# Putting VectorE and ScalarE into program order from item 3 on, with one piece of side work behind each part of the first product

## The chip, the cores and the metric

The kernel runs on one core of a Trainium2 chip. The core has a matrix engine (TensorE, PE in the profile; its weight loads are listed as PEld), three engines for elementwise work (VectorE or DVE, ScalarE or ACT, GpSimd or POOL) and SyncE (SP), which issues most of the transfers. All engines run at the same time, each through its own list of instructions in order, and wait for each other by semaphores. The metric is the time of one execution on the device in microseconds (us), as the median of several runs.

## The reference

A channel attention over four batches gives a matrix of 14592 rows of 256, and a mixture of 16 experts is applied to it: each row goes to one expert, picked by two softmaxes.

```python
B, N, C = (4, 3648, 256)
qn = q / (np.linalg.norm(q, axis=1, keepdims=True) + 1e-06)
kn = k / (np.linalg.norm(k, axis=1, keepdims=True) + 1e-06)
s = kn.transpose(0, 2, 1) @ qn / tau
a = softmax(s); x = (v @ a).reshape(B * S, D)
...
for g in range(G):            # 4 groups
    for e in range(Eg):       # 4 experts in each
        h = np.maximum(xg[mask_e] @ w1[g, e], 0.0)     # 256 -> 1024
        ye = h @ w2[g, e]                              # 1024 -> 256
        out[tok_idx] = combined[:, None] * ye
```

Everything is fp32, and the output is one row of 256 for each of the 14592 tokens.

## The kernel before

The first quarter of the time computes the attention and the routing, and scatters each row of x with its weight and token number into a table in HBM that is sorted by expert. This stage is not touched by the change.

The rest is the experts. The rows of an expert are cut into *items* of 512 rows; there are 28 (`NBIG`), numbered i = 0 to 27. An item loads its expert's w1 and w2 (1 MB each, tiles `wraw`) and its rows (`xg`). For the accuracy of fp32 each operand is split into a rounded high part and the rest (`wh`, `wl`, `xth`, `xtl`, `hh`, `hl`), and each product is made of three matmuls: high by high, high by low, low by high. Splitting a weight takes a ScalarE copy (`wh`, line 637) and a VectorE subtraction (`wl`, line 638) for each half of 128x1024.

An item has eight *parts* f = 0 to 7 of 128 hidden channels. For each part `ffn1` (line 772) multiplies the rows by a part of w1 with six matmuls of 512 columns into `hmm`; ScalarE makes `hh` from it (line 776) and VectorE `hl` (line 777). `ffn2` (line 788) multiplies that part by w2 with twelve matmuls of 256 columns into two accumulators `yacc`. It runs two parts behind (`lag`): after the first product of part f comes the second product of part f - 2. So two parts into the next item an item is finished: ScalarE and VectorE evacuate an accumulator each (`ys`, lines 795 and 797) and GpSimd scatters the rows to `out` (line 798).

Beside the parts of item i the kernel prepares item i + 1: its w1 and w2 are split (`split_w`), its rows are turned (`turn_x`, line 659, a VectorE transposition from tile `xq` to `xT`) and split (`split_x`, lines 667 and 668). Item i + 2's rows are fetched by an indirect gather on GpSimd and brought into blocks by 16 small transfers on SyncE (`quads_of`, line 615, tile `xq`). Items below 4 (`KPRE`) turn their rows with TensorE instead.

Items 4 to 27 each also *host* a stage of a small product for rows left over after the items (`q_...`): four experts' rows of 32 at a time, in a cycle of four items, so that j % 4 = 0 and 1 are the first product's two stages (`qmm`, line 875) and 2 and 3 the second's (`qacc`, line 892). The stage runs in part 2. Its weights are 1 MB more for each item, in two tiles of four loads (lines 856 and 859). All weights go through one ring of three staging tiles `wraw`, in the order w2, two tiles for the small product, w1 of the item after: each load waits until the tile three before it has been used.

The order of instructions on an engine comes from a list scheduler, which goes by the order of the program, by priorities and by its own estimate of times. `tc.manual_schedule` takes engines out of that: they run in program order. Before the change SyncE, GpSimd and TensorE are so ordered from item 3 on (lines 1002 to 1004: n counts parts, UN0 is 4), while VectorE and ScalarE are ordered by the scheduler.

Of the kernel before, what the change touches and what calls it, by code (L numbers as in the profile page):

```python
# [18 lines left out]
B, NT, C = 4, 3648, 256  # L19
# [18 lines left out]
KPRE = 4  # L38
NBIG = N // BIG
# [18 lines left out]
def attention_moe(ctx: ExitStack, tc, q, k, v, tau, w_group, w_expert, w1, w2, out):  # L58
# [19 lines left out]
    def ring(*shape, name):  # L78
        return rp.tile([P, *shape], F32, tag="ring", name=name, bufs=RING)
# [36 lines left out]
    slot4 = cp.tile([P, 4], F32, name="slot4")  # L116
# [14 lines left out]
    part = cp.tile([P, 1], F32, name="part")  # L131
# [344 lines left out]
    def tokens(ids, row, slot, nv, behind=None):  # L476

        keep = hp.tile(list(slot.shape), I32, tag=f"keep{slot.shape[1]}", name="keep", bufs=2)
        DVE.tensor_scalar(keep, slot, nv, -1.0, ALU.is_lt, ALU.mult)
        ins = DVE.tensor_tensor(ids, row.bitcast(I32), keep, ALU.bitwise_and)  # L480
        if behind is not None:
            tc.add_manual_dep(ins.ins, behind.ins.name,
                              mybir.DependencyInfo(mybir.DependencyClass.NoSync, mybir.DependencyReason.DATA),
                              reason="the rows are there by then")
        DVE.tensor_scalar(ids, ids, -1.0, float(NOID), ALU.mult, ALU.add)
# [124 lines left out]
    def quads_of(d):  # L610

        d["xq"] = ring(16, C // 4, name="xq")
        for q in range(4):
            for s in range(4):
                SP.dma_start(d["xq"][q * 32:(q + 1) * 32, s::4, :],  # L615
                             d["xg"][s * 32:(s + 1) * 32, :, q * 64:(q + 1) * 64])

    ET = mybir.EngineType
# [18 lines left out]
        ACT.activation(whs[n][:, s], raw[:, s], AF.Copy)  # L637
        DVE.tensor_tensor(wls[n][:, s], raw[:, s], whs[n][:, s], ALU.subtract)  # L638

    def split_w(i, which):  # L640

        if not whs:
            for n in range(4):
                for l, nm in ((whs, "wh"), (wls, "wl")):
                    l.append(wp.tile([P, 2048], F32R, name=f"{nm}{n}", bufs=1) if n < 3 else None)
        if i == 1 and which == "w2":
            wq = ctx.enter_context(tc.tile_pool(name="wq", bufs=1, side="right"))
            whs[3], wls[3] = [wq.tile([P, 2048], F32R, name=nm, bufs=1) for nm in ("wh3", "wl3")]
        d = items[i]
        raw = d.pop(which + "r")  # L650
        n = 2 * (i % 2) + (which == "w2")
        for c in range(2):
            split_half(raw.rearrange("p c f -> p (c f)"), n, c)
        for k, t in (("h", whs[n]), ("l", wls[n])):
            d[which + k] = t.rearrange("p (c f) -> p c f", c=raw.shape[1])

    def turn_x(d):
        d["xT"] = ring(2, BIG, name="xT")
        DVE.transpose(d["xT"].rearrange("p c (t b) -> p t c b", b=32),
                      d["xq"].rearrange("p t (a c) -> p t c a", c=2))  # L660

    def split_x(d):
        w = BIG
        xh = tp.tile([P, 2, w], F32R, tag="th", name="xth")
        xl = tp.tile([P, 2, w], F32R, tag="tl", name="xtl")
        if "xT" in d:
            ACT.activation(xh, d["xT"], AF.Copy)
            ins = DVE.tensor_tensor(xl, d["xT"], xh, ALU.subtract)
        for c in range(2) if "xT" not in d else ():
            tr = ps.tile([P, 512], F32, tag="tr", name="xtr")  # L670
            for t in range(4):
                PE.transpose(tr[:, t * P:(t + 1) * P], half(d["xg"][:, t, 0:C], c), ident)
            ACT.activation(xh[:, c, :], tr[:, :w], AF.Copy)
            ins = DVE.tensor_tensor(xl[:, c, :], tr[:, :w], xh[:, c, :], ALU.subtract)  # L674
        d["xh"], d["xl"] = xh, xl
        d["ids"] = hp.tile([P, 4], I32, tag="ids", name="ids", bufs=4)
        tokens(d["ids"], d["xg"][:, :, C], slot4, d["nv"], None if d is items[0] else ins)

    items = [dict() for _ in range(NBIG)]

# [19 lines left out]
    for t in range(len(xs_at)):  # L700
# [38 lines left out]
        if x == UX - 2:  # L739
            split_w(0, "w1")  # L740
# [25 lines left out]
    def ffn1(d, f):  # L766
        mm = ps.tile([P, 512], F32, tag="mm", name="hmm", bufs=3)
        fs = slice(f * P, (f + 1) * P)
        n = 0
        for c in range(2):  # L770
            for wt, xt in ((d["w1h"], d["xh"]), (d["w1h"], d["xl"]), (d["w1l"], d["xh"])):
                PE.matmul(mm, wt[:, c, fs], xt[:, c, :], start=(n == 0), stop=(n == 5))  # L772
                n += 1
        hh = hp.tile([P, 512], F32R, tag="hh", name="hh")
        hl = hp.tile([P, 512], F32R, tag="hl", name="hl")
        ACT.activation(hh, mm, AF.Relu)  # L776
        d["hl"] = DVE.scalar_tensor_tensor(hl, mm, 0.0, hh, ALU.max, ALU.subtract)  # L777
        d["h", f] = hh, hl
# [34 lines left out]
    def fetch_big(i, which):  # L813
        d, tb, k = where(i)
        fetch_w(d, tb, k, which)
# [47 lines left out]
    def q_xT(q, behind):  # L863
        pxt = ps.tile([P, 512], F32, tag="tr", name="qxt")
        for c in range(2):
            PE.transpose(pxt[:, c * P:(c + 1) * P], half(qs["xg"][q % 2][:, 0:C], c), ident)
        ACT.activation(qs["xT"][q % 2].rearrange("p c n -> p (c n)"), pxt[:, 0:2 * P], AF.Copy)
        tokens(qs["ids"][q % 2], qs["xg"][q % 2][:, C:C + 1], slotq, tb_pc[1][:, q:q + 1], behind)
# [126 lines left out]
    for n in range(len(seq) + lag):  # L995
        if n == 1:
            fetch_w(items[1], tb_pre, 1, "w1")
            fetch_w(items[1], tb_pre, 1, "w2")
        if n == 2:
            ms.close()  # L1000
            ms.enter_context(tc.manual_schedule(engines={ET.SP, ET.Pool}))
        if n == 8 * (UN0 - 1):
            ms.close()
            ctx.enter_context(tc.manual_schedule(engines={ET.SP, ET.Pool, ET.PE}))
        if n < len(seq):
            i, f = seq[n]
            j, jn = host(i), host(i + 1)
            if f == 3:
                if i + 2 == KPRE:
                    advance(1000)  # L1010
                    scatter(NJ)
                    tb_big, tb_pc, tb_sub, nsub = tables_rest()
                get(i + 2, weights=jn is None)
                if jn is not None:
                    if jn == 0:
                        q_tiles()
                    if jn % 4 == 0:
                        q_rows(jn // 4)
                    q_weights(jn // 4, jn % 4, 0)
            if jn is not None and f == 5:  # L1020
                q_weights(jn // 4, jn % 4, 1)
            if f == 5 and KPRE <= i + 2 < NBIG:
                quads_of(items[i + 2])
            if jn is not None and f == 7 and i + 2 < NBIG:
                fetch_big(i + 2, "w1")
            if j is not None and f == 1 and i + 1 < NBIG:
                fetch_big(i + 1, "w2")
            if j is not None and j % 4 == 0 and f == 1:
                q_xT(j // 4, items[i]["hl"])
            if i + 1 < NBIG:  # L1030
                if f == 2 and i + 1 >= KPRE:
                    turn_x(items[i + 1])
                if f == 3:
                    split_x(items[i + 1])
                if f == (4 if j is None else 5):
                    split_w(i + 1, "w1")
                if f == (6 if j is None else 7):
                    split_w(i + 1, "w2")
            if i == NBIG - 1 and f == 4:
                ns = nc.values_load(nsub[0:1, 0:1], min_val=0, max_val=NSUB)  # L1040
            ffn1(items[i], f)
            if j is not None:
                q, k = j // 4, j % 4
                if f == 2:
                    (q_ffn1 if k < 2 else q_ffn2)(q, k % 2)
                if f == 4 and k < 2:
                    q_hT(q, k)
                if f == 3 and k == 3:
                    q_put(q)
        if lag <= n < len(seq):  # L1050
            i, f = seq[n - lag]
            ffn2(items[i], f)
            if f == 7:
                finish(items[i])
        if n == len(seq) + lag - 1:

            d = items[NBIG - 1]
            d["ys"] = ring(4, C, name="ys")
            for t in (0, 2, 1, 3):
                for f in range(8 - lag, 8):  # L1060
                    ffn2(d, f, [t])
                put(d, t, d["acc"][t // 2][:, t % 2, :], t // 2)
        if n >= 1:
            advance(20 if n >= 3 else 1)
            scatter(8)
# [86 lines left out]
```

## Time and profile before

| | us |
|---|---|
| median of 3 runs | 1013.89 |
| lowest and highest | 1009.99, 1016.67 |
| the profiled execution | 1012.64 |
| its span, first to last instruction | 1010.6 |
| start of items 0, 3, 4, 8, 27 (first matmul) in the span | 257.8, 332.1, 358.4, 458.1, 968.7 |

A profile row of a group or a time line gives the engine, the line of the kernel, the operation, what it writes and reads (out<-in) and its shape; in a time line the start and duration stand ahead, and in brackets the idle time of the engine before it with what ended that wait. A row of windows gives the length of a stretch and for each engine its busy time with the number of instructions in it, then the granted clock of TensorE, the share of time in which the 16 DMA engines were busy, and GB/s. Start to start, a matmul of 512 columns takes 0.23 us there and one of 256 columns 0.12 us, though each is listed as longer: they overlap.

### The profile page before, as it was taken

What the parts mean: (1) busy time and instruction counts of PE and PEld (TensorE: products, weight loads), DVE (VectorE), ACT (ScalarE), POOL (GpSimd) and SP (SyncE); (2) the same over time, 40 slices, a digit from 0 to 9 for tenths busy, and PEclk for the clock granted to TensorE, in tenths of its full rate; (3) what the DMA queues carried; (4) which work ended last, traced back from release to release, by engine and by line L of the source; (5) the groups of instructions that cost most, each with busy time, mean ns of one, the idle gap of its engine ahead of it and who ended that gap; (6) DMA issues with size and microseconds to landing.
All of it is one profiled execution on the core that took longest, in us unless ns stands there. A gap on an engine that the chain in (4) does not pass through costs nothing.

```text
span 1010.6 us, 17899 instructions
## 1 busy us (share of the span) xinstructions
PE 952.6 (94%) x6238; PEld 819.8 (81%) x6238; DVE 612.9 (61%) x1159; ACT 472.3 (47%) x740; POOL 329.4 (33%) x425
## 2 busy tenths in 40 slices
PE   7999999988899999999999999999999999999994
PEld 6888988978788888888778777788778887777884
DVE  6989978786899555444445555554545444555551
ACT  6777677454544344334433444444443333344431
POOL 0005868886785222121112211121112111211111
PEclk9999999988999999999999999999999999999998
DMA  8857777366663466676566666676667766666650
GB/s 297 328 201 247 263 258 263 118 207 244 206 232 124 154 209 211 227 234 195 184 204 204 226 219 215 224 236 224 209 212 236 230 222 201 206 202 213 198 184 25
DMA packets 160884, 214.53 MB, mean 212 GB/s; under 512 B 65331, under 2 KB 119355, under 8 KB 160784
## 3 DMA queue, kind: packets, MB, share of 16 engines
q1 hardware_dynamic: 144352, 168.73, 51.5%
q0 software_dynamic: 14944, 44.54, 12.2%
q8 instruction: 51, 0.84, 0.3%
q14 instruction: 49, 0.40, 0.1%
q10 hardware_dynamic: 1488, 0.02, 0.1%
HBM read 170.33 MB, written 31.39 MB: 200 GB/s over the span
## 4 chain that ended last, share of the span: by engine, by line
PE 59%; DVE 9%; ACT 3%; issue 3%; DMA 2%; SPq 1%; POOL 1%; POOLq 0%; DVEq 0%; ACTq 0%
PE hmm L772 26%; PE yacc L788 25%; DVE wl L638 5%; PE qmm L875 2%; PE qacc L892 2%; PE xmm L307 2%; ACT wh L637 2%; ACT hh L776 1%; SPq L615 1%; DMA wraw<-in_moe_w 1%; DVE hl L777 1%; DMA x_sorted<-xs,si 1%; PE qtr L882 1%; DMA xg<-x_sorted,ix_big 0%; POOL out L798 0%
## 5 line engine op out<-in xcount | busy, mean ns | idle before, releaser
L777 DVE SCALAR_TENSOR_TENSOR hl<-hmm,hh 128x512 fp32r<-128x512 f32 x224 | 154.5, 690 | 309.5 <-ACT hh L776 309.5
L776 ACT ACTIVATE hh<-hmm 128x512 fp32r<-128x512 f32 x224 | 134.0, 598 | 398.0 <-PE hmm L772 376.5
L798 POOL DMA_INDIRECT out<-ys,ids x112 | 111.6, 997 | 529.4 <-ACT ys L795 501.0
L788 PE MATMUL yacc<-wh,hh 128*128 128x256 f32 x896 | 256.6, 286 | 2.4 <-DVE ys L797 2.4
L788 PE MATMUL yacc<-wh,hl 128*128 128x256 f32 x896 | 252.8, 282 | 1.2 <-DVE hl L777 1.2
L788 PE MATMUL yacc<-wl,hh 128*128 128x256 f32 x896 | 252.3, 282 | 0.0
L772 PE MATMUL hmm<-xth,wl 128*128 128x512 f32 x448 | 182.2, 407 | 13.2 <-DVE wl L638 13.2
L788 PEld LDWEIGHTS yacc<-wh,hh 128*128 128x128 f32 x896 | 168.9, 188 | 25.8 <-ACT ys L795 8.4
L772 PE MATMUL hmm<-xth,wh 128*128 128x512 f32 x448 | 180.5, 403 | 6.9 <-ACT wh L637 5.3
L772 PE MATMUL hmm<-xtl,wh 128*128 128x512 f32 x448 | 177.9, 397 | 1.9 <-DVE xtl L674 1.9
L788 PEld LDWEIGHTS yacc<-wl,hh 128*128 128x128 f32 x896 | 169.2, 189 | 8.3
L788 PEld LDWEIGHTS yacc<-wh,hl 128*128 128x128 f32 x896 | 168.8, 188 | 1.4 <-DVE hl L777 1.4
L409 POOL DMA_INDIRECT x_sorted<-xs,si x116 | 135.9, 1171 | 64.2 <-issue 37.5
L638 DVE TENSOR_TENSOR wl<-wraw,wh 128x1024 fp32r<-128x1024 f32 x112 | 131.5, 1222 | 8.5 <-ACT wh L637 7.4
L772 PEld LDWEIGHTS hmm<-xth,wl 128*128 128x128 f32 x448 | 84.6, 189 | 48.3 <-DVE wl L638 29.8
L637 ACT ACTIVATE wh<-wraw 128x1024 fp32r<-128x1024 f32 x112 | 111.0, 1050 | 12.0 <-DMA wraw<-in_moe_w 6.3
L772 PEld LDWEIGHTS hmm<-xth,wh 128*128 128x128 f32 x448 | 85.1, 190 | 20.2 <-ACT wh L637 9.2
L772 PEld LDWEIGHTS hmm<-xtl,wh 128*128 128x128 f32 x448 | 84.9, 190 | 13.0 <-DVE xtl L674 2.2
L210 PE MATMUL sacc<-qkraw 128*128 128x256 f32 (+1 forms) x352 | 86.1, 390 | 5.9 <-DMA qkraw<-in_k 5.9
L210 PEld LDWEIGHTS sacc<-qkraw 128*128 128x128 f32 (+1 forms) x352 | 65.5, 195 | 14.7 <-DMA qkraw<-in_q 5.9
L307 PE MATMUL xmm<-ahi,vth 128*128 128x276 f32 (+1 forms) x232 | 71.7, 311 | 5.2 <-ACT xs L310 4.4
L307 PE MATMUL xmm<-alo,vth 128*128 128x276 f32 (+1 forms) x232 | 70.3, 303 | 0.4 <-DVE alo L268 0.4
(233 smaller groups left out, 1190.1 us busy)
## 6 DMA issues: line engine op xcount, KB each, us to landing
wraw<-in_moe_w SPq DMA_DIRECT2D x56, 1024.0 KB
wraw<-in_moe_w SPq DMA_DIRECT2D x96, 512.0 KB
vr<-in_v SPq DMA_DIRECT2D x28, 512.0 KB
qkraw<-in_q SPq DMA_DIRECT2D x27, 512.0 KB
qkraw<-in_k SPq DMA_DIRECT2D x27, 512.0 KB
xq<-xg SPq DMA_DIRECT2D x384, 32.0 KB
xg<-x_sorted SPq DMA_DIRECT2D x4, 544.0 KB
x_sorted<-xs,si POOLq DMA_INDIRECT x116, 4.4
```

Source lines behind the costliest of these rows:

```text
L210: PE.matmul(d["acc"][:, c, :], kt[:rows, 1, cs], qt[:rows, 0, :], start=d.pop("first", True) and c == 0, stop=(g == NG), skip_group_check= ...
L307: PE.matmul(mm[:rows, :NE], vt[:, c, j * P:j * P + rows], at[:, c, :], start=(n == 0), stop=(n == 5))
L409: ins = POOL.indirect_dma_start(out=xs_d, out_offset=bass.IndirectOffsetOnAxis(ap=si[:rows, j:j + 1], axis=0), in_=xs[:rows, t, 0:RW].bitc ...
L637: ACT.activation(whs[n][:, s], raw[:, s], AF.Copy)
L638: DVE.tensor_tensor(wls[n][:, s], raw[:, s], whs[n][:, s], ALU.subtract)
L772: PE.matmul(mm, wt[:, c, fs], xt[:, c, :], start=(n == 0), stop=(n == 5))
L776: ACT.activation(hh, mm, AF.Relu)
L777: d["hl"] = DVE.scalar_tensor_tensor(hl, mm, 0.0, hh, ALU.max, ALU.subtract)
L788: PE.matmul(a, ht[:, tsl], wt[:, f, :], start=(f == 0 and t % 2 == 0 and n == 0), stop=(f == 7 and n == 2), skip_group_check=True)
L798: ins = POOL.indirect_dma_start(out=out, out_offset=bass.IndirectOffsetOnAxis(ap=d["ids"][:, t:t + 1], axis=0), in_=ys[:, t, :], in_offset ...
L875: PE.matmul(mm[r, :], qs["xT"][q % 2][:, c, r], qs["w", p][:, c * 512:(c + 1) * 512], start=(c == 0), stop=(c == 1), tile_position=(0, p * ...
L892: PE.matmul(qs["a"][r, 0:C], qs["hT"][k][:, o:o + PC], qs["w", p][:, f * C:(f + 1) * C], start=(k == 0 and f == 0), stop=(k == 1 and f == ...
```

## The change

From item 3 on VectorE and ScalarE too run in program order, and the program now says where the side work stands: one piece of it behind each part's `ffn1` (and so behind that part's `hh` and `hl`). In item i, for item i + 1: the two halves of w1 behind parts 1 and 2, the transposition of the rows behind part 3, their split behind part 4, the two halves of w2 behind parts 5 and 6. The 16 small row loads of item i + 2 are issued in part 7, behind the load of its w1, instead of in part 5 ahead of it. The masking of token numbers no longer carries an artificial order behind another instruction.

```diff
-    def split_w(i, which):
+    def split_w(i, which, part=None):
...
-        raw = d.pop(which + "r")
+        raw = d[which + "r"]
...
-        for c in range(2):
+        for c in range(2) if part is None else (part,):
...
-            ctx.enter_context(tc.manual_schedule(engines={ET.SP, ET.Pool, ET.PE}))
+            ctx.enter_context(tc.manual_schedule(engines={ET.SP, ET.Pool, ET.PE, ET.Activation, ET.DVE}))
...
-            if f == 5 and KPRE <= i + 2 < NBIG:
-                quads_of(items[i + 2])
             if jn is not None and f == 7 and i + 2 < NBIG:
                 fetch_big(i + 2, "w1")
+            if f == 7 and KPRE <= i + 2 < NBIG:
+                quads_of(items[i + 2])
...
-                q_xT(j // 4, items[i]["hl"])
+                q_xT(j // 4, None)
-            if i + 1 < NBIG:
-                if f == 2 and i + 1 >= KPRE:
-                    turn_x(items[i + 1])
+            if i + 1 < KPRE:
                 if f == 3:
                     split_x(items[i + 1])
-                if f == (4 if j is None else 5):
+                if f == 4:
                     split_w(i + 1, "w1")
-                if f == (6 if j is None else 7):
+                if f == 6:
                     split_w(i + 1, "w2")
...
             ffn1(items[i], f)
+            if KPRE <= i + 1 < NBIG:
+                if f in (1, 2):
+                    split_w(i + 1, "w1", f - 1)
+                if f == 3:
+                    turn_x(items[i + 1])
+                if f == 4:
+                    split_x(items[i + 1])
+                if f in (5, 6):
+                    split_w(i + 1, "w2", f - 5)
```

How this moves instructions, at three places. In these rows a number behind a name is that of a buffer: wh_3299 and wl_3300 hold w1 of an even item, wh_3301 and wl_3302 its w2.

ScalarE (ACT) while item 13 runs and item 14 is prepared, before; the first rows are parts 4 and 5, the last begins with part 0 of item 14:

```order
L883 ACTIVATE qhT<-qtr 128x512
L776 ACTIVATE hh<-hmm 128x512 x2
L667 ACTIVATE xth<-xT 128x1024
L776 ACTIVATE hh<-hmm 128x512
L637 ACTIVATE wh_3299<-wraw 128x1024 x2
L637 ACTIVATE wh_3301<-wraw 128x1024 x2
L776 ACTIVATE hh<-hmm 128x512 x3
```

The same engine in the same item now, from parts 7, 0 and 1 (the first row) to part 7 and the next item's parts 0 and 1 (the last):

```order
L776 ACTIVATE hh<-hmm 128x512 x3
L637 ACTIVATE wh_3299<-wraw 128x1024
L795 ACTIVATE ys<-yacc,xg 128x256 x2
L776 ACTIVATE hh<-hmm 128x512
L637 ACTIVATE wh_3299<-wraw 128x1024
L877 ACTIVATE qh_4591<-qmm 128x512
L776 ACTIVATE hh<-hmm 128x512 x2
L667 ACTIVATE xth<-xT 128x1024
L883 ACTIVATE qhT<-qtr 128x512
L776 ACTIVATE hh<-hmm 128x512
L637 ACTIVATE wh_3301<-wraw 128x1024
L776 ACTIVATE hh<-hmm 128x512
```

The four halves stood in one run behind the last hh of the item; now each stands behind an hh of its own, w1's behind parts 1 and 2 and w2's behind parts 5 and 6. VectorE's wl halves have moved in the same way.

VectorE (DVE) in parts 0 to 3 of item 3, while item 4 is prepared, before (xT, xtl: the rows of item 4; ys: item 2's results):

```order
L777 SCALAR_TENSOR_TENSOR hl<-hmm,hh 128x512 x2
L659 STREAM_TRANSPOSE xT<-xq 128x16x2x32
L797 TENSOR_SCALAR ys<-yacc,xg 128x256 x2
L638 TENSOR_TENSOR wl_3302<-wraw,wh_3301 128x1024
L777 SCALAR_TENSOR_TENSOR hl<-hmm,hh 128x512
L668 TENSOR_TENSOR xtl<-xT,xth 128x1024
```

VectorE in the same parts now:

```order
L638 TENSOR_TENSOR wl_3300<-wraw,wh_3299 128x1024
L797 TENSOR_SCALAR ys<-yacc,xg 128x256 x2
L777 SCALAR_TENSOR_TENSOR hl<-hmm,hh 128x512
L638 TENSOR_TENSOR wl_3300<-wraw,wh_3299 128x1024
L839 MEMSET qxg_4583 128x272
L839 MEMSET qxg_4584 128x272
L777 SCALAR_TENSOR_TENSOR hl<-hmm,hh 128x512
L659 STREAM_TRANSPOSE xT<-xq 128x16x2x32
L777 SCALAR_TENSOR_TENSOR hl<-hmm,hh 128x512
L668 TENSOR_TENSOR xtl<-xT,xth 128x1024
```

The transposition moved from ahead of ys to behind part 3's hl; two clearings of the small product's rows, which stood much earlier, are now in part 2; w1's halves, split before item 3 until now, stand in parts 1 and 2.

SyncE (SP) at the turn from one item to the next, before (128x2x1024 is a load of w1, 128x8x256 one of w2, 128x4x256 one of the small product's):

```order
L859 DMA wraw<-in_moe_w 128x4x256
L615 DMA xq<-xg 32x4x64 x16
L592 TENSOR_LOAD tb_big
L592 ISA x2
L595 ISA
L595 DMA wraw<-in_moe_w 128x2x1024
```

SyncE there now:

```order
L595 DMA wraw<-in_moe_w 128x2x1024
L615 DMA xq<-xg 32x4x64 x16
L592 TENSOR_LOAD tb_big
L592 ISA x2
L595 ISA
L595 DMA wraw<-in_moe_w 128x8x256
```

The 16 row loads moved past the load of w1, and stand between it and the load of w2.

More of the change, by code (lines that the diff above doesn't have):

```diff
@@ L676, in split_x @@
         d["ids"] = hp.tile([P, 4], I32, tag="ids", name="ids", bufs=4)
-        tokens(d["ids"], d["xg"][:, :, C], slot4, d["nv"], None if d is items[0] else ins)
+        tokens(d["ids"], d["xg"][:, :, C], slot4, d["nv"], None if d is items[0] or "xT" in d else ins)
     items = [dict() for _ in range(NBIG)]
```

## The prediction

> **What bounds the kernel now.** I read the page first, then the list of waits, then windows over groups of items, then the time line at one boundary between items.
>
> ```profile
> span 1010.6 us, 17899 instructions
> PE 952.6 (94%) x6238; PEld 819.8 (81%) x6238; DVE 612.9 (61%) x1159; ACT 472.3 (47%) x740; POOL 329.4 (33%) x425
> ```
>
> TensorE (PE) is busy for 94% of the span. So the question is where it stands still or runs slowly although its work is there. Items 4 to 27 all carry the same large products and, in a cycle of four, the same small ones. Windows cut at the first matmul of items 4, 8, 12, 16, 20, 24 and 27 (columns: window, length, busy us of each engine with instruction counts, granted clock, DMA share, GB/s):
>
> ```profile
> 358.40:458.10 99.70, 99.70 (x684) 85.11 (x683) 52.51 (x79) 42.69 (x64) 23.50 (x22) 1.00 0.66 222
> 458.10:564.20 106.10, 102.71 (x684) 85.81 (x682) 53.10 (x79) 42.23 (x65) 21.94 (x22) 1.00 0.67 217
> 564.20:672.30 108.10, 104.27 (x682) 85.33 (x682) 54.81 (x80) 43.69 (x66) 21.93 (x22) 1.00 0.66 216
> 672.30:780.30 108.00, 104.13 (x682) 86.06 (x682) 54.74 (x80) 43.60 (x66) 21.95 (x22) 1.00 0.68 217
> 780.30:887.90 107.60, 103.74 (x683) 85.38 (x683) 55.02 (x81) 43.65 (x66) 21.95 (x22) 1.00 0.68 220
> 887.90:968.70 80.80, 77.94 (x506) 63.92 (x506) 40.73 (x60) 33.27 (x51) 13.89 (x14) 1.00 0.66 212
> ```
>
> Four items take 99.7 us where PE has no gap, and 106 to 108 us from item 8 on, with the same number of matmuls (684 and 682) and the same clock of 1.00. That is about 2 us for each item. Two waits name the place:
>
> ```profile
> PE hmm L772 <- DVE wl L638: 13.2, 38, 0.5
> PE hmm L772 <- ACT wh L637: 5.3, 19, 0.5
> ```
>
> They come 19 times (and 2 x 19), once for each boundary from items 8/9 to 26/27. One boundary, 13/14, by parts: part 6 and 7 of item 13, part 0 and 1 of item 14:
>
> ```profile
> 613.03:615.85 2.82, 2.82 (x21) 2.55 (x19) 1.84 (x3) 1.23 (x2) 0.00 (x0) 1.00 1.07 372
> 615.85:619.11 3.26, 2.99 (x21) 2.50 (x19) 2.31 (x7) 1.92 (x4) 0.00 (x0) 1.00 0.85 299
> 619.11:623.28 4.17, 3.48 (x19) 2.52 (x20) 4.17 (x4) 3.38 (x4) 0.00 (x0) 1.00 0.17 30
> 623.28:626.10 2.82, 2.82 (x21) 2.56 (x20) 1.65 (x3) 0.60 (x1) 0.00 (x0) 1.00 1.00 342
> ```
>
> A part takes 2.82; around the boundary one takes 3.26 and one 4.17. That is 0.44 + 1.35 = 1.79 us. The time line shows why:
>
> ```profile
> 614.62 0.60 ACT L776 ACTIVATE hh<-hmm 128x512 fp32r<-128x512 f32 x1 [2.22 <-PE hmm L772]
> 617.51 0.60 ACT L776 ACTIVATE hh<-hmm 128x512 fp32r<-128x512 f32 x1 [1.34 <-PE hmm L772]
> 618.00 3.89 ACT L637 ACTIVATE wh<-wraw 128x1024 fp32r<-128x1024 f32 x4
> ...
> 619.09 4.63 DVE L638 TENSOR_TENSOR wl<-wraw,wh 128x1024 fp32r<-128x1024 f32 x4
> ...
> 619.11 0.50 PE L772 MATMUL hmm<-xth,wh 128*128 128x512 f32 x1 [0.27 <-ACT wh L637]
> 620.37 0.50 PE L772 MATMUL hmm<-xth,wl 128*128 128x512 f32 x1 [0.53 <-DVE wl L638]
> 621.50 0.50 PE L772 MATMUL hmm<-xth,wl 128*128 128x512 f32 x1 [0.16 <-DVE wl L638]
> ```
>
> The four halves of item 14's weights are split in one run, and the run begins at 618.0, in the last part of item 13. PE reaches item 14 about 1 us later.
>
> **The change, term by term.** Nothing is computed more or less often, and the order on PE and on GpSimd (POOL) stays as it was; what moves is ScalarE, VectorE and SyncE's queue. *The boundary.* The first product's weights are now split behind parts 1 and 2 of the item before, where the old order had all four halves after its last parts (the ScalarE rows shown above for item 13). That is five parts ahead of their use, and VectorE's wl halves follow in the same places. The four-item windows price the whole gain, since items 4 to 7 are the same work without these waits: 106.1 - 99.7 = 6.4, then 8.4, 8.3 and 7.9, together 31.0. Items 24 to 26 took 80.8; three such items without waits take 99.7 less the fourth:
>
> ```profile
> 433.50:458.10 24.60, 24.60 (x177) 21.22 (x177) 11.85 (x19) 9.02 (x14) 7.01 (x7) 1.00 0.60 203
> ```
>
> so 75.1, a gain of 5.7. Item 27's first part gains the 1.35 of a boundary. Sum 38.0. The 19 boundaries alone are 19 x 1.79 = 34.0; the other 4 us are small products that wait for weights, as here in item 13:
>
> ```profile
> 600.74 0.16 PEld L875 LDWEIGHTS qmm<-wraw,qxT 128*32 128x32 f32 x8 [0.78 <-DMA wraw<-in_moe_w]
> ```
>
> Their load takes the staging buffer that the first product's weights leave; with the split in parts 1 and 2 it leaves an item's half earlier. Bounds of this term: 34.0 if that does not follow, 38.0 if it does; I take 38.0, since items 4 and 5 have the same small products and took no such wait.
>
> *Item 3.* Its parts 2 and 3:
>
> ```profile
> 337.75:342.97 5.22, 3.32 (x21) 2.84 (x20) 3.19 (x6) 2.83 (x4) 2.96 (x3) 0.95 0.64 197
> 342.97:347.12 4.15, 4.15 (x20) 3.57 (x20) 2.50 (x7) 0.60 (x1) 3.34 (x3) 0.66 1.03 387
> ...
> 339.83 1.25 DVE L659 STREAM_TRANSPOSE xT<-xq 128x1024 f32<-128x1024 f32 x1 [2.03 <-DMA xq<-xg]
> 341.00 0.83 DVE L797 TENSOR_SCALAR ys<-yacc,xg 128x256 f32<-128x256 f32 x2
> ...
> 341.88 0.39 PE L788 MATMUL yacc<-wh,hh 128*128 128x256 f32 x1 [1.90 <-DVE ys L797]
> ```
>
> The transposition waits for its rows, the evacuation ys stands behind it, and PE waits for ys; then the granted clock falls to 0.66 for a part. In the new order (the VectorE rows shown above) the transposition stands behind ys and behind part 3. What is late next is ys behind one wl half: hh begins 1.6 into a part (614.62 against 613.03), wh 0.5 later, wl 1.1 after wh for 1.2, ys 0.8, so 5.2 after part 1 began and 2.4 into part 2; PE wants that accumulator some 2.0 in (an estimate: six matmuls of the first product are half of a 2.82 part, and half of the second product comes before it). Gain 5.22 + 4.15 - 2 x 2.82 - 0.4 = 3.3. The two memsets lie on VectorE between waits of PE's length; cost nothing unless VectorE is full (52.5 of 99.7 us). The Trainium skill (TensorE: Matmul & The Clock Gate, on the HAM clock gate) says that the clock halves only after an idle window of about 3.4 us. The row shows 0.66 after an idle time of 1.90 us, so here the measurement decides; by the page alone this term would be 2.0.
>
> *Items 0 to 2* are still ordered by the scheduler, and their rows on VectorE shift a little. Window 307.00:332.10 holds item 2:
>
> ```profile
> 307.00:332.10 25.10, 23.89 (x155) 21.52 (x154) 23.82 (x77) 10.68 (x17) 12.02 (x12) 1.00 0.37 119
> ```
>
> VectorE is full there and PE idles 1.2 us. I take 0, with 1.2 either way. The tail after item 27 holds evacuations and scatters in the same order: 0.
>
> Sum: 38.0 + 3.3 = 41.3 us off the profiled execution, 1012.64 - 41.3 = 971.3. The median of the runs shown is 1.25 us above that execution, so 972.6; I say 972.
>
> **What the order makes wait.** In order, a side piece whose data is late holds up hh or hl behind it. On SyncE's queue (SP) the 16 row loads xq of an item now stand behind the next item's w1 and ahead of w2. What these take:
>
> ```profile
> 326.61 11.52 SPq L615 DMA_DIRECT2D xq<-xg  x16
> 362.78 5.29 SPq L595 DMA_DIRECT2D wraw<-in_moe_w  x2
> ...
> 367.90 1.06 ACT L637 ACTIVATE wh<-wraw 128x1024 fp32r<-128x1024 f32 x1 [0.81 <-DMA wraw<-in_moe_w]
> 373.55 1.06 ACT L637 ACTIVATE wh<-wraw 128x1024 fp32r<-128x1024 f32 x1 [2.16 <-DMA wraw<-in_moe_w]
> ```
>
> A load is usable 5.1 us after its issue (362.78 to 367.90), or 5.5 after the second issue's end (368.07 to 373.55). Parts of an item of 24.7 us begin at 0, 2.8, 5.7, 10.5, 13.4, 16.2, 19.0 and 21.9 (2.82 each, and what is left of item 7's 24.60 for part 2, which holds the small product). The buffer for w1 of the item after next comes free when w2's second half is split: 19.0 + 1.6 + 0.5 + 1.1 + 1.2 = 23.4. Then w1 is usable 3.8 to 4.5 into the next item; ScalarE asks for it at 2.8 + 2.1 = 4.9. The 16 xq follow within 1 us, take 11.5 and land 1.7 after the last (338.1 to 339.83): 23.4 + 1 + 11.5 + 1.7 = 37.6, 12.9 into the next item; VectorE asks at 10.5 + 2.9 = 13.4. Then w2, issued 1.2 after the last xq and usable 5.5 later, 17.9 in; ScalarE asks at 16.2 + 2.1 = 18.3. Each is in time by 0.4 to 1.1 us. If one is late, the hh or hl behind it is late too; PE wants that only in the second product two parts on, some 4 us later (hl(4) could begin at 13.4 + 2.2 and be done by 16.3; PE asks after 19.0 + 1.4). The evacuations ys stand behind the first half in part 1, with the small product's 2 us of PE work in part 2 as their cover; without that cover, as in item 3, each us would cost a us. So I charge nothing here, and let the range carry it.
>
> **Rivals.** *The loop w1, xq, w2 becomes the bound.* Its sum is 1 + 11.5 + 1.2 + 5.5 + half a split 1.1 + hh 0.6 + half a split 2.3 = 23.2 of 24.7 us. It decides above 1.5 us more, which rows at full DMA share (342.97, 1.03) make possible; at 1 us over, 24 items give back 24: about 996. *Only PE's idle time goes*: 13.2 + 5.3 + 1.9 = 20.4 off the median, about 993; the windows of equal work speak against it. *Head-of-line blocking, slower:* xT waits in order for xq on VectorE with hl behind it, as ys stood behind it at 339.83, in every item. That price was 9.37 - 5.64 = 3.7 us; 23 times, 85, less the gain of 41 gives about 1058. It decides once xq lands over 4 us later than 13.4 in. The Trainium skill (Perfetto Trace Analysis, Per-engine timelines) states that ScalarE and VectorE are strict FIFO. The trace agrees at 341.00. *Nothing changes:* if the boundary only moves to other waits of the same length, 1014.
>
> **How the numbers follow.** Forecast (967 to 979) 0.74; loop 0.12; idle only 0.06; blocking 0.04; nothing 0.04. The range 966 to 993 leaves out the last two and the upper part of the loop case. About 1% can be told from no change: faster by more 0.91, within 0.05, slower 0.04.
>
> **What would show it.** Right: every four items from 4 on take near 99.7, part 0 takes 2.82, PE no longer waits for wl or wh, and parts 2 and 3 of item 3 take about 6. Wrong: waits of ScalarE's wh or VectorE's xT for DMA that grow over 4 us, PE waiting for hl or ys inside an item, or a granted clock under 1.00 in the denser stretch.

## The result, and the profile after

| | median us | range | executions |
|---|---|---|---|
| before | 1012.73 | 1009.99 to 1016.67 | 4 |
| changed | 973.32 | 972.45 to 978.08 | 4 |

The changed kernel takes 0.9614 of the time before (95% interval 0.9574 to 0.9654). Its profiled execution is the slowest of the four, 978.08 us, with a span of 975.9. The page's first lines:

```profile
span 975.9 us, 17902 instructions
PE 932.5 (96%) x6238; PEld 816.5 (84%) x6238; DVE 624.8 (64%) x1159; ACT 471.6 (48%) x740; POOL 341.3 (35%) x425
```

The same windows as before, four items each, cut at the first matmul of items 4, 8, 12, 16, 20, 24 and 27 (window, length, busy us of PE, PEld, DVE, ACT, POOL, granted clock, DMA share, GB/s):

```profile
361.20:460.90 99.70, 99.70 (x684) 85.14 (x683) 56.67 (x81) 43.59 (x65) 24.86 (x22) 1.00 0.71 235
460.90:560.70 99.80, 99.80 (x685) 85.24 (x684) 56.77 (x81) 43.58 (x65) 24.86 (x22) 1.00 0.72 235
560.70:660.40 99.70, 99.70 (x684) 85.14 (x683) 56.67 (x81) 43.59 (x65) 24.86 (x22) 1.00 0.72 235
660.40:760.10 99.70, 99.70 (x684) 85.14 (x683) 56.67 (x81) 43.70 (x65) 24.85 (x22) 1.00 0.72 236
760.10:859.80 99.70, 99.70 (x684) 85.14 (x683) 56.68 (x81) 43.59 (x65) 24.64 (x22) 1.00 0.72 235
859.80:934.90 75.10, 75.10 (x508) 63.92 (x508) 42.43 (x61) 33.33 (x50) 16.04 (x14) 1.00 0.70 224
```

Every window has the length of the undisturbed one, and PE's busy time fills it. From the second window on that is 6.3 + 8.4 + 8.3 + 7.9 + 5.7 = 36.6 us less than before; with 1.4 in item 27, 38.0. Now the boundary 13/14 by parts (6 and 7 of item 13, 0 and 1 of item 14), and parts 2 and 3 of item 3:

```profile
605.42:608.24 2.82, 2.82 (x20) 2.56 (x19) 1.92 (x3) 1.55 (x3) 0.00 (x0) 1.00 1.08 383
608.24:611.07 2.83, 2.83 (x20) 2.55 (x19) 1.98 (x3) 0.98 (x2) 0.00 (x0) 1.00 0.50 142
611.07:613.88 2.81, 2.81 (x20) 2.55 (x19) 0.69 (x2) 0.60 (x1) 0.00 (x0) 1.00 0.86 302
613.88:616.71 2.83, 2.83 (x20) 2.55 (x19) 0.69 (x2) 1.23 (x2) 0.00 (x0) 1.00 0.57 148
343.84:347.08 3.24, 3.08 (x20) 2.61 (x19) 2.78 (x6) 2.59 (x5) 1.97 (x2) 1.00 0.63 195
347.08:349.90 2.82, 2.82 (x20) 2.55 (x19) 2.32 (x4) 0.60 (x1) 2.21 (x3) 1.00 0.85 268
```

The parts of 3.26 and 4.17 are gone, and item 3 spends 6.06 us in two parts that took 9.37; the clock stays at 1.00 there. The list of waits has no line of PE for wl or wh any more. What it has for the weights and the evacuations:

```profile
DVE wl L638 <- ACT wh L637: 22.2, 87, 0.9
ACT wh L637 <- DMA wraw<-in_moe_w: 3.6, 2, 3.4
PE yacc L788 <- DVE ys L797: 3.1, 3, 1.8
```

The time line of the loads and of parts 1 and 2 of item 14, which begins at 611.07 with part 2 at 616.71:

```profile
609.90 0.37 SPq L595 DMA_DIRECT2D wraw<-in_moe_w  x1
610.46 10.95 SPq L615 DMA_DIRECT2D xq<-xg  x16
...
615.98 1.05 ACT L637 ACTIVATE wh<-wraw 128x1024 fp32r<-128x1024 f32 x1
...
618.21 0.87 DVE L797 TENSOR_SCALAR ys<-yacc,xg 128x256 f32<-128x256 f32 x2
```

ScalarE takes w1 up 4.9 into the item, as soon as hh is done and without a wait for the load; ys is done 2.4 into part 2.

Against the span of 1010.6 the profiled executions differ by 34.7 us. Of this 38.0 + 3.3 are items 3 to 27; items 0 to 2 take 2.1 more (76.4 against 74.3), the first item starts 4.0 later (261.8 against 257.8), and the tail takes some 0.5 more. The start is very probably no part of the change: in a later run the same kernel began item 0 at 255.1, and the kernels of all fourteen traces begin it between 255.1 and 261.8.

### The profile page after: what moved, and what is told of

It is laid out like the page before. It is cut to its first block, busy times and chain, and to the rows that moved or that the text cites. A ratio compares the mean times of both kernels' runs of the same rounds, so it can differ in the third digit from the quotient of the medians.

```text
span 975.9 us, 17902 instructions
## 1 busy us (share of the span) xinstructions
PE 932.5 (96%) x6238; PEld 816.5 (84%) x6238; DVE 624.8 (64%) x1159; ACT 471.6 (48%) x740; POOL 341.3 (35%) x425
## 4 chain that ended last, share of the span: by engine, by line
PE 69%; DVE 5%; issue 2%; POOL 1%; ACT 0%; POOLq 0%; DVEq 0%; ACTq 0%
PE yacc L788 31%; PE hmm L772 30%; PE qacc L892 2%; PE qmm L875 2%; PE xmm L307 2%; DVE hl L777 1%; DVE wl L638 1%; PE qtr L882 1%; POOL x_sorted L409 0%; PE vtr L288 0%; DVE vtl L290 0%; POOL out L798 0%; DVE ys L797 0%; PE xtr L672 0%; DVE xtl L674 0%
## 5 line engine op out<-in xcount | busy, mean ns | idle before, releaser
L798 POOL DMA_INDIRECT out<-ys,ids x112 | 128.6, 1148 | 471.9 <-ACT ys L795 444.3
L772 PE MATMUL hmm<-xth,wh 128*128 128x512 f32 x448 | 178.3, 398 | 1.6 <-ACT xth L673 1.6
L772 PE MATMUL hmm<-xth,wl 128*128 128x512 f32 x448 | 177.9, 397 | 0.0
L409 POOL DMA_INDIRECT x_sorted<-xs,si x116 | 131.3, 1132 | 71.4 <-issue 44.9
L638 DVE TENSOR_TENSOR wl<-wraw,wh 128x1024 fp32r<-128x1024 f32 x112 | 137.0, 1224 | 24.7 <-ACT wh L637 22.2
L637 ACT ACTIVATE wh<-wraw 128x1024 fp32r<-128x1024 f32 x112 | 117.4, 1052 | 5.7 <-DMA wraw<-in_moe_w 3.6
```

The lines of the kernel that those rows point to most:

```text
L409: ins = POOL.indirect_dma_start(out=xs_d, out_offset=bass.IndirectOffsetOnAxis(ap=si[:rows, j:j + 1], axis=0), in_=xs[:rows, t, 0:RW].bitc ...
L798: ins = POOL.indirect_dma_start(out=out, out_offset=bass.IndirectOffsetOnAxis(ap=d["ids"][:, t:t + 1], axis=0), in_=ys[:, t, :], in_offset ...
```

## The experiments

The runs were made in three batches of four, each on another chip, with the kernel before in each. It took 1011.27 us on the first chip, 1032.24 on the second and 1029.02 on the third. Times are compared within a batch, and across batches by the ratio to the kernel before or by windows of the traces.

**The order alone** (first batch). The places of before, with VectorE and ScalarE in program order from item 3 on:

```
-ctx.enter_context(tc.manual_schedule(engines={ET.SP, ET.Pool, ET.PE}))
+ctx.enter_context(tc.manual_schedule(engines={ET.SP, ET.Pool, ET.PE, ET.Activation, ET.DVE}))
-tokens(..., None if d is items[0] else ins)
+tokens(..., None if d is items[0] or "xT" in d else ins)
-q_xT(j // 4, items[i]["hl"])
+q_xT(j // 4, None)
```

> The old places (the first product's weights in one piece ahead of part 5, the second's ahead of part 7, rows turned in part 2, the row loads xq ahead of w1 on SyncE's queue), but VectorE and ScalarE in program order from item 3 on. Theory A, the order alone is what was missing: before, the weights of item 14 were there at about 612.6 (issue 607.53 and 5.1) and their split began at 618.0, behind xth and xtl. In program order it begins behind hh of part 4, about 15.6 into the item, and is over by 18.8, well ahead of 24.7. xT is asked for 6.7 in and its rows land about 8.5 in, a wait of 1.8 with only hl behind it, which PE wants some 4 us later. So four items take 99.7 to 100 from item 4 on, and the time is 971 to 977. Rival B, one piece behind one part is what matters: the run of two halves holds up hh and hl by 2.1 and 2.5 us in two parts of every item, and part of it reaches PE: 0.5 to 1 us for 23 items, 985 to 997. Rival C, the new places are what matters and the order nothing: 1000 to 1013.

972.25 us, 0.962 of before (0.9601 to 0.9638): the whole gain. Its first window of four items, and VectorE in item 13 (which begins at 579.42; part 5 begins at 596.05):

```profile
354.60:454.40 99.80, 99.80 (x685) 85.22 (x684) 55.30 (x81) 44.38 (x65) 22.91 (x22) 1.00 0.72 235
```
```profile
588.24 1.25 DVE L659 STREAM_TRANSPOSE xT<-xq 128x1024 f32<-128x1024 f32 x1 [2.08 <-DMA xq<-xg]
589.41 0.65 DVE L777 SCALAR_TENSOR_TENSOR hl<-hmm,hh 128x512 fp32r<-128x512 f32 x1
...
596.50 2.36 DVE L638 TENSOR_TENSOR wl<-wraw,wh 128x1024 fp32r<-128x1024 f32 x2 [0.74 <-ACT wh L637]
598.78 0.69 DVE L777 SCALAR_TENSOR_TENSOR hl<-hmm,hh 128x512 fp32r<-128x512 f32 x1
```

Both halves of w1 are split in one run of 2.36 us, done 19.4 into the item, 5.7 us ahead of their use. xT waits 2.08 with hl behind it, and PE waits for neither. Rivals B and C fall: where the kernel before takes 1011 to 1013 us, the new places are worth nothing beside the order.

**The places alone** (first batch): the changed kernel with the first two lines of that diff taken back, so that the scheduler orders both engines.

> The new places in the program, but VectorE and ScalarE left to the scheduler as before. In the order that it gives, the first product's weights are split behind part 2 (out of the boundary), but from item 9 on xT stands behind hl of part 6, xth behind hh of part 7 and xtl behind hl of part 7. Theory A, the place alone does not do: xth then begins 2.2 into part 7 and ends 0.4 into the next item, xtl ends 1.7 into it, and PE asks for xtl 0.4 to 0.9 in: about 1.3 us for each of 18 boundaries, 23 us, so 973 + 23 = 996 (992 to 1003), with PE waiting for VectorE's xtl and ScalarE's xth instead of wl and wh, and items 4 to 8 at 24.9 as in the changed kernel. Rival B, an early split is all that counts: 972 to 978.

1088.85 us, 1.077 of before (1.0749 to 1.0786): neither theory. The boundary waits came as forecast, but most of the loss was one that no theory had. The list of waits and VectorE's time line in item 13 (part 6 begins at 650.1):

```profile
DVE ids L480 <- DMA xg<-x_sorted,ix_big: 170.1, 21, 11.1
PE yacc L788 <- DVE hl L777: 53.3, 24, 5.1
```
```profile
653.65 0.16 DVE L480 TENSOR_TENSOR ids<-xg,keep 128x4 int32<-128x4 int32 x1 [9.55 <-DMA xg<-x_sorted,ix_big]
...
654.06 1.88 DVE L777 SCALAR_TENSOR_TENSOR hl<-hmm,hh 128x512 fp32r<-128x512 f32 x3
```

An operation of 0.16 us waits 9.55 for rows that are still being gathered, and three hl stand behind it. The hint that the change drops had kept ids behind xtl.

**The places, with that hint kept** (second batch):

```
-tokens(..., None if d is items[0] or "xT" in d else ins)
+tokens(..., None if d is items[0] else ins)
```

> The new places with VectorE and ScalarE left to the scheduler, as in the run of the places alone, but with the one hint kept that the changed kernel drops: the token numbers ids of an item are worked out behind its xtl. In the run without the hint the scheduler put ids, which needs a gather of rows xg issued in part 4, ahead of hl of part 4, and VectorE waited 170 us in all for it (21 times, about 8 each). Theory A: that wait is what made that run slower, and what is left is xth and xtl late at the boundary, 1.1 to 1.5 us (part 0 took 3.96 there instead of 2.82, the last part 3.19) for 18 boundaries: 973 + 25 = 998 (990 to 1003). Rival B: it is the places themselves that clash with the scheduler's order; the time stays over 1040. Rival C: 972 to 978, the places alone do it.

1035.95 us beside 1032.24 of before, 1.005 (1.0022 to 1.0081), where the run without the hint had 1.077. So Theory A was right on ids, which is most of the loss, and wrong on what is left: it said 990 to 1003, under the kernel before. xth and xtl are late at the boundary (part 0 takes 3.8 in the mean of items 6 to 25, the last part 3.1), and the scheduler has more of the same kind. ScalarE in part 2 of item 13:

```profile
609.33 0.60 ACT L877 ACTIVATE qh<-qmm 128x512 f32<-128x512 f32 x1 [1.31 <-PE qmm L875]
609.83 0.83 ACT L795 ACTIVATE ys<-yacc,xg 128x256 f32<-128x256 f32 x2
```

ys, whose accumulator is long complete, stands behind qh, which waits for the small product; PE then waits 1.5 us for ys (13.2 us in all, 9 times).

**One engine alone** (third batch): the order-alone kernel with only ET.DVE, and with only ET.Activation, added to the list of engines.

> The old places, with VectorE in program order from item 3 on and ScalarE left to the scheduler. In the order that this gives, VectorE has xtl behind hl of part 2, while ScalarE has xth, which it needs, behind hh of part 4, so hl of parts 3 and 4 stand behind an xtl that is done about 2.2 into part 5. PE asks for hl of part 3 about 1.4 into part 5. Theory A, the two orders have to agree: 1.5 us or more for each of 23 items, 1000 to 1020, PE waiting for VectorE's hl in part 5 of every item. Rival B, VectorE's order is the one that matters: 971 to 978.

> The old places, with ScalarE in program order from item 3 on and VectorE left to the scheduler. The scheduler then gives VectorE nearly the order of the program: xT and xtl behind hl of part 2, wl of the first product behind hl of part 4, of the second behind hl of part 6, but ids one item ahead, behind hl of part 6, at about the time its gather lands. Theory A: 971 to 980, four items in 99.7 to 101. Rival B, both engines have to be told: 990 or more.

VectorE alone: 1018.32 us, 0.9912 of before (0.9878 to 0.9945). The waits say why:

```profile
DVE xtl L668 <- ACT xth L667: 121.6, 24, 8.3
PE yacc L788 <- DVE hl L777: 21.9, 22, 1.0
```

VectorE stands some 5 us in every item for an xth that ScalarE has two parts later, and hl behind it reaches PE 1 us late, 22 times; part 5 takes 4.1 us. That is Theory A. ScalarE alone: 992.2 us, 0.9653 (0.9607 to 0.9699); the scheduler then gives VectorE nearly the order of the program. By its number that is Rival B, 12 us over Theory A's range. But PE's waits for hl are 3.4 us in all here, and most of what it takes above the changed kernel is in part 3 (3.5 us in the mean of items 6 to 25, 2.8 in the changed kernel), with gaps that the last experiment tells of and that both engines in order had too on this chip. So what VectorE's order adds to ScalarE's is not settled.

**Halves or wholes, and w2 one part later** (first batch):

```
-                if f in (1, 2):
-                    split_w(i + 1, "w1", f - 1)
+                if f == 1:
+                    split_w(i + 1, "w1")
...
-                if f in (5, 6):
-                    split_w(i + 1, "w2", f - 5)
+                if f == 5:
+                    split_w(i + 1, "w2")
```

> The changed kernel, with both halves of w1 behind part 1 and both of w2 behind part 5, in place of one half behind each of two parts. The VectorE evacuation ys then stands behind two halves, 1.2 us later: done about 3.6 into part 2, where PE wants it about 4.0 in. w1's buffer comes free 2.8 earlier. Theory A, the one-piece rule is worth nothing while the small product covers ys: 972 to 977, item 3 (without a small product) longer by 1.2. Rival B, pieces of half the size are needed: ys 1.2 late in every item, 23 times, 28 us: about 1000.

973.23 us, 0.9631 (0.9613 to 0.965): Theory A. Items 4 to 7 take 99.75 us, and item 3 24.15 against 23.01, the 1.1 us that nothing covers there. Then, in place of this, the two halves of w2 behind parts 6 and 7:

> The changed kernel, with the halves of w2 behind parts 6 and 7 instead of 5 and 6. The staging buffer for w1 of the item after next comes free 2.8 later: the changed kernel issues that load 23.8 in (609.90 of item 13), which becomes 26.6, so w1 is usable about 7.0 into the next item, and ScalarE asks for it at 4.9: 2.1 late. The evacuation ys stands behind that half; it is done 2.4 into part 2, and PE wants it about 4.0 in, behind the small product. Theory A, each term has its own slack: 2.1 less 1.6 gives 0.5 us for each of 23 items, 12 us, so about 985 (978 to 990). Rival B, all waits are within the tolerance: 972 to 976. Rival C, the loop of loads becomes the bound: 2 to 2.8 us for every item, 1020 to 1040.

981.58 us, 0.9714 (0.9695 to 0.9733): Theory A. ScalarE's wait for the load, and the first window of four items:

```profile
ACT wh L637 <- DMA wraw<-in_moe_w: 47.3, 24, 3.3
```
```profile
353.20:455.00 101.80, 100.48 (x684) 85.37 (x683) 56.38 (x81) 43.48 (x66) 23.96 (x22) 1.00 0.69 227
```

w1 comes 2.0 us late in each item (47.3 / 24), and an item grows by about 0.4 (items 4 to 26 take 583.3 us, 573.8 in the changed kernel). So the cover of ys is 1.6 us; the loop of loads is no bound.

**The rows turned earlier** (second batch). The same wait for xq, with different work behind it: turn_x behind hl of part 1 (ahead of ys), and behind hl of part 2 (after ys):

```
+                if f == 1:                      # f == 2 in the other
+                    turn_x(items[i + 1])
                 if f in (1, 2):
                     split_w(i + 1, "w1", f - 1)
-                if f == 3:
-                    turn_x(items[i + 1])
```

> The changed kernel, with the transposition xT two parts earlier: behind hl of part 1, ahead of the first half of w1 and of the evacuation ys. VectorE asks for it 5.7 into the item; the last of the 16 row loads is issued 9.7 in and lands about 11.5 to 12. Theory A, head-of-line blocking with a cover of its own: VectorE waits about 6 us for xq, ys is done about 9.8 into part 2 rather than 2.4, PE wants it about 4.0 in: 5.8 us for each of 23 items, and 1.2 more where the clock falls behind such a stall (parts of 4.0 instead of 2.8 came behind stalls of 4 to 5 us in the run of the places alone): 1100 to 1140. Rival B, VectorE has room (64% busy) and the wait is covered: 972 to 980.

> The changed kernel, with the transposition xT one part earlier: behind hl of part 2 and ys, ahead of the second half of w1. VectorE asks for it 8.7 into the item, xq lands 11.5 to 12 in, so it waits about 3 us there in every item. Behind it stand only wl and hl of part 3; hl is then done about 14.8 in, and PE asks for it after 16.2. Theory A: a wait of the same kind costs nothing where only hl stands behind it: 971 to 977, with some 65 us of waits of VectorE for xq. Rival B, each wait of VectorE for a load costs its length: 3 us for 23 items, about 1040.

Ahead of ys: 1141.35 us, 1.107 of before (1.1001 to 1.1147). VectorE in item 14, and PE behind it:

```profile
695.19 1.24 DVE L659 STREAM_TRANSPOSE xT<-xq 128x1024 f32<-128x1024 f32 x1 [6.79 <-DMA xq<-xg]
696.36 1.18 DVE L638 TENSOR_TENSOR wl<-wraw,wh 128x1024 fp32r<-128x1024 f32 x1
697.46 0.86 DVE L797 TENSOR_SCALAR ys<-yacc,xg 128x256 f32<-128x256 f32 x2
```
```profile
698.38 0.58 PE L788 MATMUL yacc<-wh,hh 128*128 128x256 f32 x1 [5.76 <-DVE ys L797]
```

After ys: 984.36 us, 0.954 (0.9474 to 0.9607). VectorE in item 13, which begins at 586.9:

```profile
598.90 1.25 DVE L659 STREAM_TRANSPOSE xT<-xq 128x1024 f32<-128x1024 f32 x1 [3.38 <-DMA xq<-xg]
```

It waits 3.4 us here, 2.6 to 4.6 in the items from 4 on, and PE never waits for hl. Ahead of ys VectorE waits 5.3 to 7.1 in the same items, and PE 5.1 in the mean (117.4 us, 23 times); there the clock falls behind many of these stalls, and part 3 takes 4.1 in the mean instead of 2.8. So the run ahead of ys is Theory A, just over its range. Its wait is also longer, since it is asked for 2.9 earlier. That length is not the whole difference: with w2 one part later, 2.0 us late ahead of ys cost 0.4, and here up to 4.6 ahead of hl cost nothing. The run after ys is 7 us above Theory A, though not by these waits; see the last experiment.

**The rows loaded first** (second batch): quads_of back at f == 5, ahead of the w1 of f == 7 on SyncE's queue.

> The changed kernel, with the 16 row loads xq back at part 5, ahead of the next w1 on SyncE's queue, as before. They wait for the gather of xg, which lands about 1.8 into part 6 (20.8 into the item), take 10.7 to issue, and w1 is issued behind them 6.8 into the next item and usable 12 in; ScalarE asks for it at 4.9: about 7 us late, with ys behind its first half. In the run with w2 one part later a w1 late by 2.0 cost 0.35 us an item. Theory A, the queue's order is part of the change and the new places need it: 5.4 us for 23 items and 1.2 more where the clock falls: 1090 to 1130. Rival B, w1 is issued early enough either way: 972 to 980.

1095.52 us, 1.0623 (1.0556 to 1.069): Theory A. PE waits above all for ScalarE's ys, which stands behind the late half of w1:

```profile
ACT wh L637 <- DMA wraw<-in_moe_w: 132.9, 24, 8.7
PE yacc L788 <- ACT ys L795: 78.8, 23, 6.5
```

The new places of w1 only work with the queue's new order; the old places (the order alone) work with the old one.

**A candidate, and the changed kernel beside it** (third batch). The order alone, with ys of items 0 to 2 on ScalarE:

```
-put(d, t, d["acc"][t // 2][:, t % 2, :], t // 2)
+put(d, t, d["acc"][t // 2][:, t % 2, :], 0 if any(d is o for o in items[:3]) else t // 2)
```

> The order alone with the old places (972.25), and for items 0 to 2 all four evacuations ys on ScalarE in place of two on ScalarE and two on VectorE. In items 1 and 2 of the run with the order alone PE stood 2.05 and 1.74 us for VectorE's ys, behind the tables that VectorE works out there. Theory A: ScalarE is free there, ys is done in time, and 3 to 4 us go: 0.996 to 0.997 of the changed kernel. Rival B: VectorE is full in items 1 and 2, and something else that it does (hl) is late by as much: no difference.

> The changed kernel as it is, for comparison with the others on the same chip: 0.957 to 0.966 of before, four items in 99.7 us from item 4 on.

The changed kernel: 973.30 us, 0.9477 of before (0.9441 to 0.9514). The candidate: 987.26, 0.9605 (0.9559 to 0.9651), so 1.014 of the changed kernel where less than 1 was expected. Items 0 to 2 take 74.0 us in it and 75.8 in the changed kernel: item 1 lost its wait for ys, while in item 2 PE waits 1.2 and 0.3 us for hl instead, so about half of Theory A. But later items are longer, with gaps of PE for which the trace shows no releaser. The candidate, then the changed kernel:

```profile
PE hmm L772 <- issue: 7.7, 17, 0.9
PE yacc L788 <- issue: 3.5, 6, 1.1
```
```profile
PE hmm L772 <- issue: 0.5, 1, 0.5
PE yacc L788 <- issue: 0.4, 1, 0.4
```

11.2 us against 0.9. Nearly all lie in parts 2 and 3 of items 6, 7, 10, 11 and so on, most of them while a w1 of 1024 KB is coming in. In their earlier runs neither the order alone nor the changed kernel shows one. The runs with one engine alone in order and with the rows turned behind part 2 show them too. From item 4 on the candidate has the instructions of the order alone in the same order on PE, VectorE, ScalarE and GpSimd, so there it stands for that kernel, which was not itself run on this chip. Its items 4 to 26 take 593.3 us, 575.4 in the changed kernel. So on this chip the new places are worth some 16 to 18 us beside the order, and on the first nothing. What makes PE stand in the gaps, and why the kernel before is slower by 18 to 21 us on the later chips, is open. The changed kernel took 973.3 us in both of its runs, and nothing that was run is faster by more than the noise.

## Why the prediction came out

- *The bound* (windows of equal work) was read rightly: 99.7 us per four items before and after.
- *The boundary, 38.0 us:* 38.0 measured, the upper end; the small products' waits went too. But the reason named only half of it. The prediction put the gain on the split "behind parts 1 and 2 of the item before". The order-alone run splits w1 behind part 4, where the program had it all along, and gains the same. The scheduler had moved the split behind part 7, and taking that away is the change; the places alone lost 78 us against before. On the third chip the places seem to matter beside the order, for a reason that is open.
- *Item 3, 3.3 us:* 26.32 to 23.01 us; part 2 is 0.42 over 2.82 by the wait for ys, where 0.4 was said.
- *Items 0 to 2, "0, with 1.2 either way":* this step failed. They cost 2.1 us in the profiled execution and 1.5 in the later one of the same kernel. In the profiled one 0.9 of it is item 0, where the mean granted clock was 0.87 and not 0.93; the later one has 0.93 there. What both show is items 1 and 2, longer by 1.2 and 1.7 us, with PE waiting up to 1.9 for ys behind VectorE's tables. A shifted order of the scheduler on a full engine was priced at nothing; it should have had a price of the size of such a wait.
- *The slack:* the loads came as worked out (16 row loads in 10.95 us against 11.5; xq there 12.0 us into item 13 in the run that waits for it, 11.3 to 13.5 over the items, 12.9 forecast). "Their cover" for ys, 2 us, measured as 1.6.
- *Head-of-line blocking:* rightly a minor rival for this change, and real as a mechanism. It was put at 1058 us; a wait ahead of ys gave 1141. The condition "over 4 us later" fits a wait with hl behind it as far as that was tried, since waits of up to 4.6 us cost nothing; with ys behind it, it is 1.6. The Trainium skill (Perfetto Trace Analysis, Per-engine timelines) has ScalarE and VectorE as strict FIFO, and 653.65 and 695.19 agree.
- *The loop as the bound, and only PE's idle time:* the first is refuted by the later w2 (0.4 us an item, through ys), the second by the windows.

The total fell within 2 us of the forecast because the sum was taken from windows of equal work, which need no right answer to what had moved the split. That it came so near is in part luck: the start of item 0 alone differs by 6.7 us between the traces, and the profiled execution missed its own 971.3 by 6.8.

## What to carry to other kernels

Price a removed wait by stretches of the same work with and without it; that holds even where the reason is not yet clear. Where a queue runs in order, ask of each instruction that may wait what stands behind it and when that is needed: a wait of 2.6 to 4.6 us cost nothing ahead of hl, and one of 5.3 to 7.1 us cost 5.1 ahead of ys. When an order is fixed by hand or a hint is dropped, do it for all engines that hand work to each other: VectorE alone gave 1018 us where both, with ys of items 0 to 2 moved, gave 987 in the same batch.

## What the hardware did unexpectedly

The clock behind a stall does not follow from the stall's length. Before, it fell behind 1.90 us (341.88 in the prediction's rows). Behind 1.89 us in item 1 of the order-alone run, and then behind 3.30 us in item 3 of the places with the hint, it stayed:

```profile
290.77 0.39 PE L788 MATMUL yacc<-wh,hh 128*128 128x256 f32 x1 [1.89 <-DVE ys L797]
```
```profile
353.26 0.39 PE L788 MATMUL yacc<-wh,hl 128*128 128x256 f32 x1 [3.30 <-DVE hl L777]
```

The traces show what decides. In all fourteen the granted clock is 1.00 or 0.50, and from its first change on each whole stretch at one of the two is a multiple of 3.413 us: the clock changes on a fixed grid. The 0.66 of the kernel before is the mean of a part; the clock itself was 0.50 for 3.41 us. The windows of that grid around the three stalls, for before, the order alone, and the places with the hint:

```profile
338.99:342.41 3.42, 1.52 (x12) 1.27 (x11) 2.58 (x4) 1.34 (x3) 1.69 (x3) 1.00 0.75 235
342.41:345.82 3.41, 3.41 (x12) 2.83 (x12) 2.37 (x4) 0.27 (x2) 2.61 (x3) 0.50 0.99 359
```
```profile
289.10:292.52 3.42, 1.75 (x15) 1.75 (x15) 3.42 (x7) 0.26 (x1) 2.98 (x6) 1.00 0.93 318
292.52:295.93 3.41, 3.41 (x23) 3.07 (x22) 3.41 (x11) 1.43 (x3) 3.08 (x5) 1.00 0.41 135
```
```profile
348.28:351.69 3.41, 1.68 (x9) 1.22 (x7) 0.00 (x0) 0.60 (x1) 0.00 (x0) 1.00 0.82 335
351.69:355.10 3.41, 1.84 (x13) 1.76 (x14) 2.39 (x8) 0.00 (x0) 0.00 (x0) 1.00 0.21 47
355.10:358.52 3.42, 3.42 (x22) 3.03 (x21) 2.22 (x3) 2.49 (x3) 0.00 (x0) 1.00 0.19 39
```

The stall before lies whole in one window, in which PE idles 56% of the time, and the next window runs at 0.50. The other two are cut by an edge of the grid: their windows idle 49% at most in the one and 51% in the other, and the clock stays. From 262 us on, the fourteen traces have 2934 such windows at 1.00. Each with PE idle for over 54.5% of it was followed by a fall, none with under 47.5% was, and between the two it went either way. So where a stall falls decides as much as how long it is.

The Trainium skill (TensorE: Matmul & The Clock Gate, on the HAM clock gate) has a window of 3.4 us that runs freely. The traces agree, with the 3.413 us above. The other surprise is PE's gaps without a releaser in the later batches, told of above.
